# Linear attention with a token mixer: k'v matmuls and q' transposes in 64-row tiles, two PSUM banks each

## The chip, the cores and the metric

The kernel runs on one core of a Trainium2 chip. The metric is the device time of one execution in microseconds (us). Times of a kernel are medians of several executions; a profile is of one execution. Runs come with a state, fast or slow, and with the mean clock that the throttle granted TensorE (1.00 is full speed). On this one core the clock varied from run to run for one and the same kernel: among seven executions of the kernel before on one chip, 177.44 us went with a clock of 0.941 and 185.43 us with 0.892. Fast runs are compared with fast runs. The state is set among runs taken side by side, though: beside e5 to e8 all seven runs of the kernel before lie between 180.51 and 182.86 us (clock 0.897 to 0.926) and count as fast, where runs of that length beside e1 to e4 counted as slow.

## The reference

```python
# attention, per batch (8) and head (8); 576 positions s, 64 dims
q_p = concat(relu(q) * cos_w, relu(q) * sin_w)     # (s, 128), k_p likewise
kv  = einsum('bhsf,bhsd->bhfd', k_p, v)            # contraction over s
z   = sum(k_p, axis=s)
x   = einsum('bhsf,bhfd->bhsd', q_p, kv) / (q_p . z + 1e-6)
# token mixer on x (b, s, 512)
W = (x @ w_q) @ (x @ w_k).T / 8;   out = relu(W @ x) @ w_out
```

## The kernel before

Two heads (a pair) share the 128 partitions: the 576 positions of one head lie on partitions 0 to 63 in nine chunks, those of the other on 64 to 127. To keep the heads apart in a contraction over all 128 rows, `v_ext` holds each head's v beside a block of zeros; a column of ones next to v gives z.

```python
for pr in range(NPAIR):                                  # 4 pairs of heads
    kv_sb = small.tile([P, 2, D + 1], BF16, name="kv_sb")
    qpt_ps = psum.tile([P, C9, P], BF16, name="qpt_ps", bufs=1)        # 2 banks
    kv_ps = psum.tile([P, 2, D + 1], FP32, name="kv_ps", bufs=1)       # 1 bank
    for c in range(C9):                                  # 9 chunks
        nc.tensor.matmul(kv_ps, k_p[:, pr, c, :, :], v_ext[:, pr, c, :, :],
                         start=(c == 0), stop=(c == C9 - 1))
    # (kv_sb <- kv_ps)
    for c in range(C9):
        nc.tensor.transpose(qpt_ps[:, c, :], q_p[:, pr, c, :, :], ident)
    # (qpt_sb <- qpt_ps, on VectorE)
    for hh in range(2):                                  # the two heads
        num_ps = psum.tile([P, SC, D + 1], FP32, name="num_ps", bufs=2)  # 2 banks
        for u in range(SC):                              # 5 slices of 128 positions
            nc.tensor.matmul(num_ps[:, u, :], qpt_sb[:, hh, cb:cb + 2, :],
                             kv_sb[:, hh, :], start=True, stop=True)
        nc.vector.reciprocal(rec, num_ps[:, :, D:D + 1])
        nc.vector.tensor_tensor(x_sb[:, :, h, :], num_ps[:, :, 0:D],
                                rec.to_broadcast([P, SC, D]), op=ALU.mult)
```

The mixer's tiles (`xT_ps`, `moe_ps_a` to `moe_ps_e`) share a pool of three banks. With qpt_ps 2, kv_ps 1 and num_ps 2 all eight banks are taken. A scheduler fixes the order of the instructions on each engine when the kernel is built; on the chip each engine then follows that order.

Of the kernel before, what the change touches and what calls it, by code (L numbers as in the profile page):

```python
# [14 lines left out]
FP32 = mybir.dt.float32  # L15
BF16 = mybir.dt.bfloat16
# [6 lines left out]
def kernel(  # L23
# [10 lines left out]
    nc = tc.nc  # L34

    B, H, S, D = q.shape
    DM = H * D
    DH = moe_w_q.shape[1]
    P = 128
    NPAIR = H // 2  # L40
    C9 = (2 * S) // P
    NDM = DM // P
    SC = S // P + 1
    scale_moe = 1.0 / math.sqrt(DH)

    consts = ctx.enter_context(tc.tile_pool(name="consts", bufs=1))
# [7 lines left out]
    psum = ctx.enter_context(tc.tile_pool(name="psum", bufs=1, space=bass.MemoryType.PSUM))  # L54
# [7 lines left out]
    ident = consts.tile([P, P], BF16)  # L62
# [34 lines left out]

    v_bufs = []
    for i in range(2):
        vb = consts.tile([P, NPAIR, C9, 2, D + 1], BF16, name=f"v_buf{i}")  # L100
        for hh in range(2):
            p0 = hh * 64
            eng = nc.vector if hh == 0 else nc.gpsimd
            eng.memset(vb[p0:p0 + 64, :, :, 1 - hh, :], 0.0)
            eng.memset(vb[p0:p0 + 64, :, :, hh, D:D + 1], 1.0)
        v_bufs.append(vb)

    num_slices = [(i * P, P) for i in range(4)] + [(S - P, P)]
# [3 lines left out]
    def attention(b, x_sb, nsplit):  # L112
        qf = inp.tile([P, NPAIR, C9 * D], FP32, name="qf")
        kf = inp.tile([P, NPAIR, C9 * D], FP32, name="kf")
        vf = inp.tile([P, NPAIR, C9 * D], FP32, name="vf")
        rq = work.tile([P, NPAIR, C9, D], BF16, name="rq", bufs=1)
        rk = work.tile([P, NPAIR, C9, D], BF16, name="rk", bufs=1)
        q_p = work.tile([P, NPAIR, C9, 2, D], BF16, name="q_p")
        k_p = work.tile([P, NPAIR, C9, 2, D], BF16, name="k_p")
        v_ext = v_bufs[b % 2]  # L120

        step = NPAIR // nsplit
        for sp in range(nsplit):
            a, bb = sp * step, (sp + 1) * step
            csb = cossin.unsqueeze(1).to_broadcast([P, step, C9, 2, D])
            for dst, rr, pp, src in ((kf, rk, k_p, k), (vf, None, None, v),
                                     (qf, rq, q_p, q)):
                s4 = src[b].flatten().rearrange(
                    "(pr p e) -> p pr e", pr=NPAIR, p=P)
                nc.sync.dma_start(dst[:, a:bb, :], s4[:, a:bb, :])  # L130
                if rr is None:
                    for hh in range(2):
                        p0 = hh * 64
                        for pr in range(a, bb):
                            nc.gpsimd.tensor_copy(  # L135
                                v_ext[p0:p0 + 64, pr, :, hh, 0:D],
                                dst[p0:p0 + 64, pr, :].rearrange(
                                    "p (c d) -> p c d", c=C9))
                else:
                    nc.any.tensor_scalar(rr[:, a:bb, :, :], dst[:, a:bb, :],  # L140
                                         0.0, None, op0=ALU.max)
                    nc.vector.tensor_mul(  # L142
                        pp[:, a:bb, :, :, :],
                        rr[:, a:bb, :, :].unsqueeze(3).to_broadcast(
                            [P, step, C9, 2, D]),
                        csb)

        for pr in range(NPAIR):
            kv_sb = small.tile([P, 2, D + 1], BF16, name="kv_sb")
            qpt_ps = psum.tile([P, C9, P], BF16, name="qpt_ps", bufs=1)  # L150
            kv_ps = psum.tile([P, 2, D + 1], FP32, name="kv_ps", bufs=1)
            for c in range(C9):
                nc.tensor.matmul(  # L153
                    kv_ps,
                    k_p[:, pr, c, :, :],
                    v_ext[:, pr, c, :, :],
                    start=(c == 0),
                    stop=(c == C9 - 1),
                )
            with tc.high_priority(2000):  # L160
                nc.any.tensor_copy(kv_sb, kv_ps)  # L161
            for c in range(C9):
                nc.tensor.transpose(  # L163
                    qpt_ps[:, c, :], q_p[:, pr, c, :, :], ident)
            qpt_sb = small.tile([P, 2, C9, D], BF16, name="qpt_sb")
            with tc.high_priority(2000):
                nc.vector.tensor_copy(  # L167
                    qpt_sb, qpt_ps.rearrange("f c (hh pp) -> f hh c pp", hh=2))

            for hh in range(2):  # L170
                h = 2 * pr + hh
                num_ps = psum.tile([P, SC, D + 1], FP32, name="num_ps", bufs=2)
                for u in range(SC):
                    cb = cbase_of[u]
                    nc.tensor.matmul(  # L175
                        num_ps[:, u, :],
                        qpt_sb[:, hh, cb:cb + 2, :],
                        kv_sb[:, hh, :],
                        start=True,
                        stop=True,  # L180
                    )
                rec = small.tile([P, SC, 1], FP32, name="rec")
                nc.vector.reciprocal(rec, num_ps[:, :, D:D + 1])
                nc.vector.tensor_tensor(  # L184
                    x_sb[:, :, h, :],
                    num_ps[:, :, 0:D],
                    rec.to_broadcast([P, SC, D]),
                    op=ALU.mult,
                )
# [88 lines left out]
    for b in range(B):  # L278
        x_sb = xpool.tile([P, SC, H, D], BF16, name="x_sb")
        attention(b, x_sb, 4 if b == 0 else 2)  # L280
        if b % 2 == 0:
            mix_sb = mixpool.tile([P, NDM, 2 * S], BF16, name="mix_sb")
            mix_keep = mix_sb
        else:
            mix_sb = mix_keep
        moe_front(b, x_sb, mix_sb, b % 2)
        if b % 2 == 1:
            wout(b - 1, mix_sb)
# [30 lines left out]
```

## Time and profile before

| | before |
|---|---|
| time, first three executions | 177.77 us (176.94 to 178.58) |
| granted clock of the profiled run | 0.932 |
| TensorE (PE) busy | 147.2 us, 83% |
| VectorE (DVE) busy | 134.1 us, 75% |
| ScalarE (ACT), GpSimd (POOL) busy | 89.9 and 56.6 us |

For the argument about buffers, two groups of the page's fifth part are needed too (line, engine, operation, names, shape, count; then busy us, mean ns; then idle time just before them, with what ended it):

```profile
L175 PE MATMUL num_ps<-kv_sb,qpt_sb 128*128 128x65 bf16 x320 | 21.3, 196 | 3.0 <-DVE x_sb L184 1.5
...
L135 POOL CAST v_buf<-vf 64x576 bf16<-64x576 f32 x64 | 51.2, 822 | 71.9 <-DMA vf<-in_v_dram 33.4
```

and a piece of the timeline of the kernel before (start us, us, instruction, count):

```profile
106.16 0.31 PE L175 MATMUL num_ps<-kv_sb,qpt_sb 128*128 128x65 bf16 x5
...
106.55 0.32 PE L175 MATMUL num_ps<-kv_sb,qpt_sb 128*128 128x65 bf16 x5
...
107.00 0.25 DVE L183 RECIPROCAL rec<-num_ps 128x5 f32<-128x5 f32 x2
...
107.21 0.89 DVE L184 TENSOR_TENSOR x_sb<-num_ps,rec 128x320 bf16<-128x320 f32 x2
```

TensorE does both heads of a pair within 0.7 us and hardly ever waits for a division (1.5 us in all). VectorE takes both reciprocals and both products together when it gets to them, 0.84 us after the first head began. Two buffers make that possible.

### The profile page before, as it was taken

The page shows a single profiled execution, that of the slowest core. Times are in us where ns is not written, and L with a number is a line of the kernel's source. Part 1 is how long each engine was busy: PE and PEld are TensorE (multiplying, and loading weights), DVE is VectorE, ACT ScalarE, POOL GpSimd, SP SyncE. Part 2 cuts the span into 40 slices and gives each one's busy share as a digit, 9 for nine tenths or more (in the row PEclk, how much of TensorE's full clock was granted, in tenths as well). Part 3 has the DMA queues.
Part 4 walks back from the last instruction along what each step waited for, and adds up shares of the span by engine and source line. Part 5 has one row for each costly group of instructions (what it writes and reads, how often), then busy time and mean ns, then how long its engine had stood idle before and what let it go on. Part 6 is the DMA issues. An engine that isn't in the chain of part 4 may idle for free.

```text
span 178.0 us, 3706 instructions
## 1 busy us (share of the span) xinstructions
PE 147.2 (83%) x1434; PEld 90.6 (51%) x1434; DVE 134.1 (75%) x279; ACT 89.9 (51%) x167; POOL 56.6 (32%) x75
## 2 busy tenths in 40 slices
PE   6920776889958999999989999998999999759930
PEld 2300774656645446875745467675544756423410
DVE  5827989869999899897799999879994976722000
ACT  3028155148607869525496862491885426033630
POOL 8636283887882300000576000145800000000000
PEclk9995579579999999999999999999999999996996
DMA  6999999999792038789990587999008850000886
GB/s 172 312 393 315 382 397 392 391 392 388 256 387 109 2 80 186 166 220 398 397 385 37 130 204 170 292 400 389 19 0 195 205 135 0 4 0 0 189 201 140
DMA packets 20513, 39.30 MB, mean 221 GB/s; under 512 B 3088, under 2 KB 3088, under 8 KB 20496
## 3 DMA queue, kind: packets, MB, share of 16 engines
q1 hardware_dynamic: 18912, 37.76, 66.7%
q10 hardware_dynamic: 1584, 1.31, 2.5%
q8 instruction: 11, 0.18, 0.4%
q14 instruction: 6, 0.05, 0.1%
HBM read 29.62 MB, written 9.44 MB: 219 GB/s over the span
## 4 chain that ended last, share of the span: by engine, by line
PE 56%; DVE 17%; ACT 10%; DMA 8%; issue 4%; SPq 1%; POOL 0%; ACTq 0%
PE moe_ps_e L260 10%; PE kv_ps L153 10%; PE qpt_ps L163 9%; PE moe_ps_d L242 6%; PE moe_ps_c L229 5%; PE xT_ps L196 5%; PE num_ps L175 5%; DMA qf<-in_q_dram 5%; DVE k_p L142 5%; PE moe_ps_a L207 4%; DVE q_p L142 3%; DVE qpt_sb L167 3%; DVE x_sb L184 3%; ACT wqkT_sb L214 2%; DMA wq_f<-in_moe_w_q_dram 2%
## 5 line engine op out<-in xcount | busy, mean ns | idle before, releaser
L135 POOL CAST v_buf<-vf 64x576 bf16<-64x576 f32 x64 | 51.2, 822 | 71.9 <-DMA vf<-in_v_dram 33.4
L163 PE MATMUL qpt_ps<-ident,q_p 128*128 128x128 bf16 x288 | 29.8, 228 | 10.5 <-DVE q_p L142 9.4
L260 PE MATMUL moe_ps_e<-wo_sb,mix_sb 128*128 128x512 bf16 x144 | 33.9, 391 | 0.3
L153 PE MATMUL kv_ps<-v_buf,k_p 128*128 128x130 bf16 x288 | 29.0, 235 | 2.0 <-ACT kv_sb L161 0.8
L184 DVE TENSOR_TENSOR x_sb<-num_ps,rec 128x320 bf16<-128x320 f32 x64 | 29.8, 481 | 0.1
L167 DVE COPY qpt_sb<-qpt_ps 128x1152 bf16<-128x1152 bf16 x32 | 24.1, 754 | 4.7 <-PE qpt_ps L163 4.2
L268 ACT COPY o_sb<-moe_ps_e 128x512 f32<-128x512 f32 x34 | 19.9, 586 | 13.5 <-PE moe_ps_e L260 7.2
L163 PEld LDWEIGHTS <-q_p 128*128 128x128 bf16 x288 | 19.1, 102 | 14.9 <-DVE q_p L142 10.7
L175 PE MATMUL num_ps<-kv_sb,qpt_sb 128*128 128x65 bf16 x320 | 21.3, 196 | 3.0 <-DVE x_sb L184 1.5
L142 DVE TENSOR_TENSOR k_p<-rk,cossin 128x2304 bf16<-128x2304 bf16 (+1 forms) x18 | 23.3, 1297 | 0.2 <-ACT rk L140 0.2
L140 ACT ACTIVATE rk<-kf 128x1152 bf16<-128x1152 f32 (+1 forms) x17 | 17.7, 1048 | 11.1 <-DVE k_p L142 5.6
L142 DVE TENSOR_TENSOR q_p<-rq,cossin 128x2304 bf16<-128x2304 bf16 (+1 forms) x18 | 23.2, 1290 | 0.0
L260 PEld LDWEIGHTS <-mix_sb 128*128 128x128 bf16 x144 | 14.1, 100 | 17.0 <-issue 2.6
L153 PEld LDWEIGHTS <-k_p 128*128 128x128 bf16 x288 | 19.7, 105 | 5.3 <-ACT kv_sb L161 1.7
L249 ACT ACTIVATE mix_sb<-moe_ps_d 128x512 bf16<-128x512 f32 (+1 forms) x50 | 19.3, 441 | 5.1 <-PE moe_ps_d L242 4.7
L161 ACT CAST kv_sb<-kv_ps 128x130 bf16<-128x130 f32 x24 | 6.4, 268 | 28.0 <-PE kv_ps L153 28.0
L175 PEld LDWEIGHTS <-qpt_sb 128*128 128x128 bf16 x320 | 15.6, 99 | 9.4 <-issue 2.5
L140 ACT ACTIVATE rq<-qf 128x1152 bf16<-128x1152 f32 (+1 forms) x17 | 18.3, 1080 | 3.4 <-DMA qf<-in_q_dram 3.0
L196 PE MATMUL xT_ps<-ident,x_sb 128*128 128x128 bf16 (+1 forms) x160 | 17.4, 220 | 1.3 <-DVE x_sb L184 1.1
L242 PE MATMUL moe_ps_d<-wqkT_sb,kx_sb 64*128 64x512 bf16 x64 | 14.9, 288 | 1.1 <-ACT kx_sb L237 0.7
L201 DVE COPY xT_sb<-xT_ps 128x576 bf16<-128x576 bf16 x32 | 13.4, 441 | 2.4 <-PE xT_ps L196 2.2
L196 PEld LDWEIGHTS <-x_sb 128*128 128x128 bf16 (+1 forms) x160 | 11.6, 99 | 5.1 <-DVE x_sb L184 1.2
(45 smaller groups left out, 103.0 us busy)
## 6 DMA issues: line engine op xcount, KB each, us to landing
out_dram<-o_sb SPq DMA_DIRECT2D x72, 128.0 KB, 2.4
kf<-in_k_dram SPq DMA_DIRECT2D x14, 576.0 KB, 9.5
vf<-in_v_dram SPq DMA_DIRECT2D x14, 576.0 KB, 9.5
qf<-in_q_dram SPq DMA_DIRECT2D x14, 576.0 KB, 10.5
kf<-in_k_dram SPq DMA_DIRECT2D x4, 288.0 KB, 5.4
vf<-in_v_dram SPq DMA_DIRECT2D x4, 288.0 KB, 6.2
qf<-in_q_dram SPq DMA_DIRECT2D x4, 288.0 KB, 7.5
wo_f<-in_moe_w_out_dram ACTq DMA_DIRECT2D x1, 1024.0 KB, 10.7
```

Source lines behind the costliest of these rows:

```text
L135: nc.gpsimd.tensor_copy(v_ext[p0:p0 + 64, pr, :, hh, 0:D], dst[p0:p0 + 64, pr, :].rearrange("p (c d) -> p c d", c=C9))
L140: nc.any.tensor_scalar(rr[:, a:bb, :, :], dst[:, a:bb, :], 0.0, None, op0=ALU.max)
L142: nc.vector.tensor_mul(pp[:, a:bb, :, :, :], rr[:, a:bb, :, :].unsqueeze(3).to_broadcast([P, step, C9, 2, D]), csb)
L153: nc.tensor.matmul(kv_ps, k_p[:, pr, c, :, :], v_ext[:, pr, c, :, :], start=(c == 0), stop=(c == C9 - 1),)
L163: nc.tensor.transpose(qpt_ps[:, c, :], q_p[:, pr, c, :, :], ident)
L167: nc.vector.tensor_copy(qpt_sb, qpt_ps.rearrange("f c (hh pp) -> f hh c pp", hh=2))
L175: nc.tensor.matmul(num_ps[:, u, :], qpt_sb[:, hh, cb:cb + 2, :], kv_sb[:, hh, :], start=True, stop=True,)
L184: nc.vector.tensor_tensor(x_sb[:, :, h, :], num_ps[:, :, 0:D], rec.to_broadcast([P, SC, D]), op=ALU.mult,)
L196: nc.tensor.transpose(xT_ps[:, j0:j0 + npn], x_sb[p0:p0 + npn, u, 2 * hp:2 * hp + 2, :], ident[p0:p0 + npn, p0:p0 + npn],)
L242: nc.tensor.matmul(mx_ps[:, 0:nn], kx_sb[:, dmc * P:(dmc + 1) * P], wqkT_sb[0:64, n0:n0 + nn], start=True, stop=True,)
L260: nc.tensor.matmul(o_ps, mix_sb[:, dmc, rt * P:(rt + 1) * P], wo_sb[:, dmc, :], start=(dmc == 0), stop=(dmc == NDM - 1),)
L268: nc.any.tensor_copy(o_sb, o_ps)
```

## The change

The intent: rows 0 to 63 and 64 to 127 of the array become two tiles that work side by side, one head each. The zeros beside v go, with the memsets that wrote them; 18 casts on all 128 partitions take the place of 64 on 64 partitions; and TensorE should need half the time for kv and the transposes. So that each row tile writes to a bank of its own (the rule is cited in the prediction below), kv_ps gets a second bank, which is taken from num_ps.

```diff
-            eng.memset(vb[p0:p0 + 64, :, :, 1 - hh, :], 0.0)     # and the ones, per half
+        nc.gpsimd.memset(vb[:, :, :, D:D + 1], 1.0)
 ...
-                    for hh in range(2):  ... for pr in range(a, bb):  64-partition casts
+                    nc.gpsimd.tensor_copy(v_ext[:, a:bb, :, 0:D], dst[:, a:bb, :]...)
 ...
-            qpt_ps = psum.tile([P, C9, P], BF16, name="qpt_ps", bufs=1)
-            kv_ps = psum.tile([P, 2, D + 1], FP32, name="kv_ps", bufs=1)
+            qpt_ps = psum.tile([P, 2, 1024], BF16, name="qpt_ps", bufs=1)
+            kv_ps = psum.tile([P, 2, 512], FP32, name="kv_ps", bufs=1)
             for c in range(C9):
-                nc.tensor.matmul(kv_ps, k_p[:, pr, c, :, :], v_ext[:, pr, c, :, :], ...)
+                for hh in range(2):
+                    p0 = hh * 64
+                    nc.tensor.matmul(kv_ps[:, hh, 0:D + 1],
+                                     k_p[p0:p0 + 64, pr, c, :, :],
+                                     v_ext[p0:p0 + 64, pr, c, :], ...)
 ...
-                nc.tensor.transpose(qpt_ps[:, c, :], q_p[:, pr, c, :, :], ident)
+                for hh in range(2):
+                    nc.tensor.transpose(qpt_ps[:, hh, c * D:(c + 1) * D],
+                                        q_p[p0:p0 + 64, pr, c, :, :],
+                                        ident[p0:p0 + 64, p0:p0 + 64])
 ...
-                num_ps = psum.tile([P, SC, D + 1], FP32, name="num_ps", bufs=2)
+                num_ps = psum.tile([P, SC, D + 1], FP32, name="num_ps", bufs=1)
```

More of the change, by code (lines that the diff above doesn't have):

```diff
@@ L99 @@
     for i in range(2):
-        vb = consts.tile([P, NPAIR, C9, 2, D + 1], BF16, name=f"v_buf{i}")
-        for hh in range(2):
-            p0 = hh * 64
-            eng = nc.vector if hh == 0 else nc.gpsimd
-            eng.memset(vb[p0:p0 + 64, :, :, 1 - hh, :], 0.0)
-            eng.memset(vb[p0:p0 + 64, :, :, hh, D:D + 1], 1.0)
+        vb = consts.tile([P, NPAIR, C9, D + 1], BF16, name=f"v_buf{i}")
+        nc.gpsimd.memset(vb[:, :, :, D:D + 1], 1.0)
         v_bufs.append(vb)
@@ L131, in attention @@
                 if rr is None:
-                    for hh in range(2):
-                        p0 = hh * 64
-                        for pr in range(a, bb):
-                            nc.gpsimd.tensor_copy(
-                                v_ext[p0:p0 + 64, pr, :, hh, 0:D],
-                                dst[p0:p0 + 64, pr, :].rearrange(
-                                    "p (c d) -> p c d", c=C9))
+                    nc.gpsimd.tensor_copy(
+                        v_ext[:, a:bb, :, 0:D],
+                        dst[:, a:bb, :].rearrange("p pr (c d) -> p pr c d", c=C9))
                 else:
@@ L149, in attention @@
             kv_sb = small.tile([P, 2, D + 1], BF16, name="kv_sb")
-            qpt_ps = psum.tile([P, C9, P], BF16, name="qpt_ps", bufs=1)
-            kv_ps = psum.tile([P, 2, D + 1], FP32, name="kv_ps", bufs=1)
+            qpt_ps = psum.tile([P, 2, 1024], BF16, name="qpt_ps", bufs=1)
+            kv_ps = psum.tile([P, 2, 512], FP32, name="kv_ps", bufs=1)
             for c in range(C9):
-                nc.tensor.matmul(
-                    kv_ps,
-                    k_p[:, pr, c, :, :],
-                    v_ext[:, pr, c, :, :],
-                    start=(c == 0),
-                    stop=(c == C9 - 1),
-                )
+                for hh in range(2):
+                    p0 = hh * 64
+                    nc.tensor.matmul(
+                        kv_ps[:, hh, 0:D + 1],
+                        k_p[p0:p0 + 64, pr, c, :, :],
+                        v_ext[p0:p0 + 64, pr, c, :],
+                        start=(c == 0),
+                        stop=(c == C9 - 1),
+                    )
             with tc.high_priority(2000):
-                nc.any.tensor_copy(kv_sb, kv_ps)
+                nc.any.tensor_copy(kv_sb, kv_ps[:, :, 0:D + 1])
             for c in range(C9):
-                nc.tensor.transpose(
-                    qpt_ps[:, c, :], q_p[:, pr, c, :, :], ident)
+                for hh in range(2):
+                    p0 = hh * 64
+                    nc.tensor.transpose(
+                        qpt_ps[:, hh, c * D:(c + 1) * D],
+                        q_p[p0:p0 + 64, pr, c, :, :],
+                        ident[p0:p0 + 64, p0:p0 + 64])
             qpt_sb = small.tile([P, 2, C9, D], BF16, name="qpt_sb")
@@ L167, in attention @@
                 nc.vector.tensor_copy(
-                    qpt_sb, qpt_ps.rearrange("f c (hh pp) -> f hh c pp", hh=2))
+                    qpt_sb.rearrange("f hh c pp -> f hh (c pp)"),
+                    qpt_ps[:, :, 0:C9 * D])
             for hh in range(2):
                 h = 2 * pr + hh
-                num_ps = psum.tile([P, SC, D + 1], FP32, name="num_ps", bufs=2)
+                num_ps = psum.tile([P, SC, D + 1], FP32, name="num_ps", bufs=1)
                 for u in range(SC):
```

## The prediction

> **What bounds the kernel now.** I read the page first, for the share of each engine and the chain of work that ended last; then the busy times by stage; then single instructions in the timeline, for the pace of the matmuls that change. The page's first part, its slices of TensorE and its granted clock, and its chain:
>
> ```profile
> PE 147.2 (83%) x1434; PEld 90.6 (51%) x1434; DVE 134.1 (75%) x279; ACT 89.9 (51%) x167; POOL 56.6 (32%) x75
> ...
> PE   6920776889958999999989999998999999759930
> ...
> PEclk9995579579999999999999999999999999996996
> ...
> PE 56%; DVE 17%; ACT 10%; DMA 8%; issue 4%; SPq 1%; POOL 0%; ACTq 0%
> PE moe_ps_e L260 10%; PE kv_ps L153 10%; PE qpt_ps L163 9%; PE moe_ps_d L242 6%; PE moe_ps_c L229 5%; PE xT_ps L196 5%; PE num_ps L175 5%; DMA qf<-in_q_dram 5%; DVE k_p L142 5%; PE moe_ps_a L207 4%; DVE q_p L142 3%; DVE qpt_sb L167 3%; DVE x_sb L184 3%; ACT wqkT_sb L214 2%; DMA wq_f<-in_moe_w_q_dram 2%
> ```
>
> TensorE holds 56% of the chain, and the two groups that change hold 10% and 9% of the span on it, some 34 us. By stage (PE, PEld, DVE, ACT, POOL busy, each with its count, then clock, DMA share and GB/s):
>
> ```profile
> 16.00:32.00 16.00, 10.65 (x127) 9.14 (x127) 15.42 (x31) 6.66 (x10) 8.46 (x11) 0.71 1.04 383
> ...
> 72.00:97.00 25.00, 23.44 (x287) 15.76 (x286) 21.44 (x54) 14.21 (x31) 9.00 (x12) 1.00 0.86 285
> 97.00:131.00 34.00, 32.72 (x353) 20.78 (x352) 30.98 (x63) 20.52 (x42) 8.95 (x12) 1.00 0.69 210
> 131.00:161.00 30.00, 26.80 (x251) 15.37 (x250) 20.26 (x54) 12.64 (x27) 0.00 (x0) 1.00 0.34 80
> ```
>
> From 16 to 32 us VectorE is the bound (15.42 of 16). In the steady stretch of two batches, 97 to 131, TensorE has 32.72 of 34 and VectorE 30.98: nearly level. So a faster TensorE alone can win at most the distance to VectorE, 3 us in 34, and whatever delays VectorE costs in full.
>
> The pace of the matmuls at full clock, from the timeline (start, us, then the group):
>
> ```profile
> 105.14 0.61 PE L163 MATMUL qpt_ps<-ident,q_p 128*128 128x128 bf16 x8
> 106.55 0.32 PE L175 MATMUL num_ps<-kv_sb,qpt_sb 128*128 128x65 bf16 x5
> 71.37 0.63 PE L153 MATMUL kv_ps<-v_buf,k_p 128*128 128x130 bf16 x8
> ```
>
> Less the last one's own length (0.22, 0.19 and 0.22 us by the median rows): (0.61-0.22)/7 = 56 ns for 128 columns, (0.63-0.22)/7 = 58 ns for 130, (0.32-0.19)/4 = 32 ns for 65; the records of single starts give a median of 29 ns for the last. The weight load of 128 columns hides even at 29 ns.
>
> **What the Trainium skill says.** "TensorEngine Tiling (Array Packing)", section Key Properties: tiles work independently, different tiles can load weights and multiply in parallel, and a change of tiling mode drains TensorE. The trace agrees on the drain: between adjacent matmuls it has a median of 152 ns from a 128-row one to a 64-row one and 132 ns back, against 55 and 29 ns within a mode, so about 100 ns a switch. No run here shows the parallel tiles, as the kernel before never alternates two. The same page, section Gotcha 1: PSUM Pressure: different row tiles write to different banks and may not share one. That is what the second bank is for. "TensorE: Matmul & The Clock Gate", section "Wait — 56ns, not 53.3ns?": start to start never falls below about 25 ns however few the columns; the trace's 29 ns for 64 and 65 columns lies just above it. "Perfetto Trace Analysis", section Optimization Strategy: a gap that repeats can mean that PSUM has no room for the next tile. No such gap is in the trace before; I expect it after.
>
> **The change, part by part.**
>
> 1. The kv matmuls and transposes. Removed: 288 x 58 + 288 x 56 ns = 32.8 us of TensorE. Added: 1152 of 65 or 64 columns. If they follow one another like other matmuls of that width, 1152 x 29 ns = 33.4 us: nothing gained, 0.6 us lost. If the two row tiles run side by side, half of that, 16.7 us: 16.1 us of TensorE saved. Which of the two is the main thing that I can't read from this profile. In the slow clock from 13 to 40 us the first kv groups ran at 108 ns each, and side-by-side tiles would help most there, but VectorE and the loads bound that stage.
>
> 2. Mode switches. In the instruction order of the two builds the row mode changes 170 times before and 176 times after: the 64-row work now lies next to transposes of the same mode as often as it parts from the 128-row ones. 6 x 0.1 = 0.6 us, nothing.
>
> 3. The banks. kv_ps grows from one to two, qpt_ps stays at two, moe keeps three, so num_ps falls from two buffers to one. With one, the next head's five matmuls wait until the division of this head is done. The trace gives the links: the reciprocal starts 230 ns after the start of the fifth matmul when VectorE is free, reciprocal and product end 710 ns later, and the next allowed matmul starts 55 ns after; with 120 ns for four starts, 1.1 us a head at least. 64 x 1.1 = 70 us fit in the span only if other work lies between. In the present trace 50 of 63 heads begin before the head in front is divided, so the second buffer is used. In the new order 20 of the 63 gaps between heads hold under 0.5 us of TensorE work, mostly one transpose group (0.38 us), where about 1.0 is needed: 20 x 0.6 = 12 us of TensorE waits at least, and more where VectorE first copies qpt_sb (0.76 us). In a plain attention pair of the new order I followed the steps: qpt ends, copy 0.80, reciprocal and product 0.70, next head; TensorE has 0.6 us of work and stands 0.9. VectorE in turn stands 0.4 us (55+120+230) where two heads follow with nothing between; the order has 13 such places, 5 us.
>
> 4. GpSimd. 64 casts at 822 ns become 4 of 576 and 14 of 1152 elements on all partitions. At the same time per element, 4 x 0.82 + 14 x 1.64 = 26 us instead of 51. It is off the chain, so the saving is small: one wait near 46 us for v_buf (0.7 us on the chain, up to 1.7 with the stretch before it), and four VectorE products of 1.65 to 1.87 us instead of 1.35, and four of 1.0 to 1.2 instead of 0.75, that ran beside casts: half of 3 us. Say 2 us in all.
>
> 5. The start. The two memsets of 2.0 us on VectorE and two of 2.1 on GpSimd vanish, but lie before the loads have landed. The first matmul can be kv after k_p instead of the transpose after q_p, 1.2 us sooner; half of it should remain.
>
> 6. Small shifts. The order gives VectorE 9 more 64-column and 2 more 512-column mix_sb, and 6 more wqkT_sb copies of which one is wide: 9 x 0.22 + 2 x 0.69 + 5 x 0.22 + 0.6 = 5 us, less 3 kv_sb (0.9) and one o_sb (0.7): 3.4 us more, against the 4 us of memsets that bound nothing. The attention of the last batch moves wholly in front of the third output block, so the tail of 22 us before the last block has less to do, and the stretch before it more.
>
> **The sum, for the two cases.** Steady stretch of some 120 us. *Tiles in turn:* +0.6 +0.6, waits for num_ps of 12 us of which I let two thirds reach the end (8, as the rest falls where TensorE waits anyway), VectorE +2, GpSimd -2, start -0.6: about +8, 185 to 186 us. *Tiles side by side:* 16 us of TensorE gone, but VectorE had 105 of those 120 us; with 5 us of standing and 3.4 more work, less 1.5, it has 112 and can't be packed fully: a gain of 2 to 4 us at best from TensorE, 2.6 from items 4 and 5, given back in part to the waits: -2 to -4, 174 to 176 us. I hold them about equally likely.
>
> **The rivals.** First, the full 16 us come through, 165 us. For: the chain holds 34 us of these groups. Against: VectorE's 30.98 of 34, and the chain names only what came last. Second, the single num_ps buffer decides, tiles in turn or not, 184 to 190. For: the 50 of 63 heads. Against: in-order TensorE was given an order made for one buffer, with wide gaps at 43 places. Third, alternating tiles is slower than one mode, as each weight load meets the other tile's matmul; at 40 ns, 46 us instead of 33: over 190. Nothing in the profile speaks for it.
>
> **Range and chances.** The middle of the two cases is 179.5 us, 1% above now. 171.5 holds the side-by-side case with few waits, 188 the other with most of them. The gain of over 2% needs the tiles in parallel and VectorE kept fed: 0.24. Over 2% slower needs tiles in turn, or waits larger than I let through: 0.40. Between them 0.36.
>
> **What would show it.** Start to start inside the new kv groups: 29 ns means in turn, about 15 side by side. TensorE or its weight loads idle on x_sb L184 (1.5 and 2.4 us now): near 12 us shows item 3. VectorE idle before the reciprocal on num_ps (4.3 now): near 9. v_buf casts near 26 us busy. In the stretch of two batches, TensorE well below VectorE in the first case. Wrong would be: casts slower per element, a slower granted clock, or a chain still led by TensorE at a lower total, which would mean that VectorE was less of a bound than I think.

## The result

The changed kernel takes 224.94 us (220.91 to 235.48, four runs) against 178.18 us. Its fast runs are 1.249 times those of before (95% interval 1.229 to 1.268). Such a ratio is the mean time of one kernel's fast runs over that of the other's of the same rounds, so it is not quite the ratio of the medians quoted. The profiled run is slow (226.84 us, clock 0.727), but the two fast runs had 0.730 and 0.741, and a fast run of the first experiment below shows the same structure.

The page after, its first parts and its chain:

```profile
PE 164.8 (73%) x1998; PEld 93.3 (42%) x2010; DVE 138.7 (62%) x289; ACT 87.7 (39%) x153; POOL 25.0 (11%) x27
...
PE   7707565637856889688379997987999779668960
...
PEclk9965555556955899979658999599558955555697
...
PE 44%; DVE 36%; ACT 7%; DMA 6%; issue 3%; SPq 1%; ACTq 0%; DVEq 0%
```

The clock is between one half and six tenths through much of the run, where it was near full speed after the first fifth before. VectorE's part of the chain has doubled from 17% to 36%. TensorE is busy for longer although it has less to do. By stage (columns as in the prediction):

```profile
16.00:32.00 16.00, 10.08 (x257) 8.21 (x259) 16.00 (x24) 7.21 (x11) 3.76 (x4) 0.50 1.02 384
...
97.00:131.00 34.00, 27.21 (x341) 15.81 (x343) 25.88 (x51) 16.96 (x32) 5.85 (x3) 0.82 0.46 159
131.00:161.00 30.00, 25.93 (x410) 15.45 (x410) 18.69 (x52) 7.70 (x17) 0.00 (x0) 0.81 0.26 60
```

From 97 to 131 us neither engine is near full any more: 27.21 and 25.88 of 34, where it was 32.72 and 30.98. So they wait for each other. The table of waits names it (who waited for whom: us in total, times, longest):

```profile
ACT kv_sb L155 <- PE num_ps L174: 37.5, 19, 3.8
...
DVE rec L182 <- PE num_ps L174: 24.3, 17, 9.4
PEld L174 <- DVE x_sb L183: 22.7, 33, 2.0
...
PE num_ps L174 <- DVE x_sb L183: 18.2, 32, 1.8
```

and of the kernel before:

```profile
DVE rec L183 <- PE num_ps L175: 4.3, 5, 2.5
```

TensorE's num_ps matmuls wait 18.2 us for divisions (1.5 before), the reciprocals 24.3 us for num_ps (4.3 before). The first line of the changed kernel is a second-order wait: ScalarE can't store kv_sb until a num_ps matmul has read an older one, as there are six kv_sb tiles and the kv work has run ahead of the heads. A pair in the timeline of the changed kernel:

```profile
91.99 0.47 PE L147 MATMUL kv_ps<-v_buf,k_p 64*128 64x65 bf16 x18 [0.35 <-ACT kv_sb L155]
...
93.19 0.33 PE L174 MATMUL num_ps<-kv_sb,qpt_sb 128*128 128x65 bf16 x5 [0.19 <-DVE x_sb L183]
...
93.55 0.20 DVE L182 RECIPROCAL rec<-num_ps 128x5 f32<-128x5 f32 x1 [0.42 <-PE num_ps L174]
93.78 0.49 DVE L183 TENSOR_TENSOR x_sb<-num_ps,rec 128x320 bf16<-128x320 f32 x1
...
94.33 0.33 PE L174 MATMUL num_ps<-kv_sb,qpt_sb 128*128 128x65 bf16 x5 [0.46 <-DVE x_sb L183]
94.70 0.27 ACT L155 CAST kv_sb<-kv_ps 128x130 bf16<-128x130 f32 x1 [2.27 <-PE num_ps L174]
...
95.02 0.54 PE L147 MATMUL kv_ps<-v_buf,k_p 64*128 64x65 bf16 x18 [0.36 <-ACT kv_sb L155]
```

Two things are to be seen. The tiles do work side by side: 18 matmuls in 0.47 us, less the last one's 0.20, is 16 ns from start to start, and (0.46-0.20)/17 = 15 ns in another group. That is the pace of the quickest groups: over the 24 kv groups that the trace has whole, the median is 26 ns, as 16 of them ran at a clock near 0.5. And the heads stand in a row: VectorE idle 0.42, TensorE idle 0.46, in turn, with 1.14 us from one head to the next and 3.03 us from one pair to the next. Early in the run it is worse, as VectorE's order has other work inside a division:

```profile
26.71 0.43 PE L174 MATMUL num_ps<-kv_sb,qpt_sb 128*128 128x65 bf16 x5 [0.38 <-DVE x_sb L183]
...
28.38 0.18 DVE L182 RECIPROCAL rec<-num_ps 128x5 f32<-128x5 f32 x1
28.48 1.31 DVE L134 TENSOR_TENSOR k_p<-rk,cossin 128x2304 bf16<-128x2304 bf16 x1
...
29.72 0.75 DVE L165 COPY qpt_sb<-qpt_ps 128x1152 bf16<-128x1152 bf16 x1
...
30.39 0.47 DVE L183 TENSOR_TENSOR x_sb<-num_ps,rec 128x320 bf16<-128x320 f32 x1
...
30.96 0.45 PE L174 MATMUL num_ps<-kv_sb,qpt_sb 128*128 128x65 bf16 x5
```

This head holds the buffer from 26.71 to 30.86, over 4 us.

I therefore tallied the hold in every trace: from the start of a head's first num_ps matmul to the end of the instruction that reads the buffer last.

| profiled run | num_ps buffers | mean hold | 64 holds together | next head begun before the hold ended |
|---|---|---|---|---|
| before | 2 | 2.90 us | 186 us | 50 of 63 |
| changed | 1 | 2.13 us | 136 us | 0 |
| before with one buffer (e1) | 1 | 2.09 us | 134 us | 0 |
| changed, division first (e8) | 1 | 1.77 us | 113 us | 0 |
| changed, ScalarE empties it (e7) | 1 | 1.12 us | 71 us | 0 |

With one buffer the holds can't overlap, so 136 us of the 224.8 are taken by them in a row, besides the stages in which no head is at work at all. From the first num_ps matmul to the last product it is 132.7 us before, 170.5 in e1 and 178.2 in the changed kernel: nearly all of the loss lies in the stretch of the heads. With two buffers the holds overlap, and together they cover only 113.6 us. They are also longer, as TensorE runs ahead of VectorE: between the fifth matmul and the reciprocal lie 86 us in all before and 45 in e1.

### The profile page after: what moved, and what is told of

Read it like the earlier page. It is cut to its first block, busy times and chain, and to the rows that moved or that the text cites. A ratio compares the mean times of both kernels' runs of the same rounds, so it can differ in the third digit from the quotient of the medians.

```text
span 224.8 us, 4796 instructions
## 1 busy us (share of the span) xinstructions
PE 164.8 (73%) x1998; PEld 93.3 (42%) x2010; DVE 138.7 (62%) x289; ACT 87.7 (39%) x153; POOL 25.0 (11%) x27
## 4 chain that ended last, share of the span: by engine, by line
PE 44%; DVE 36%; ACT 7%; DMA 6%; issue 3%; SPq 1%; ACTq 0%; DVEq 0%
PE moe_ps_e L259 14%; DVE x_sb L183 9%; DVE q_p L134 8%; DVE qpt_sb L165 7%; PE num_ps L174 7%; PE moe_ps_c L228 7%; DVE k_p L134 6%; PE moe_ps_a L206 6%; PE moe_ps_d L241 4%; PE xT_ps L195 4%; DMA qf<-in_q_dram 3%; ACT mix_sb L248 3%; DVE rec L182 3%; DVE xT_sb L200 2%; PE kv_ps L147 2%
## 5 line engine op out<-in xcount | busy, mean ns | idle before, releaser
L174 PE MATMUL num_ps<-kv_sb,qpt_sb 128*128 128x65 bf16 x320 | 26.5, 219 | 19.1 <-DVE x_sb L183 18.2
L128 POOL CAST v_buf<-vf 128x1152 bf16<-128x1152 f32 (+1 forms) x18 | 23.9, 1325 | 100.0 <-PE kv_ps L147 42.6
L147 PE MATMUL kv_ps<-v_buf,k_p 64*128 64x65 bf16 x576 | 22.7, 220 | 14.4 <-DVE k_p L134 10.5
L183 DVE TENSOR_TENSOR x_sb<-num_ps,rec 128x320 bf16<-128x320 f32 x64 | 31.1, 486 | 1.3
L159 PE MATMUL qpt_ps<-ident,q_p 64*128 64x64 bf16 x576 | 25.1, 216 | 6.7 <-DVE qpt_sb L165 5.4
L174 PEld LDWEIGHTS <-qpt_sb 128*128 128x128 bf16 x320 | 17.3, 111 | 29.4 <-DVE x_sb L183 22.7
L182 DVE RECIPROCAL rec<-num_ps 128x5 f32<-128x5 f32 x64 | 12.0, 188 | 24.5 <-PE num_ps L174 24.3
L147 PEld LDWEIGHTS <-k_p 64*128 64x128 bf16 x576 | 16.4, 112 | 20.2 <-DVE k_p L134 11.8
L155 ACT CAST kv_sb<-kv_ps 128x130 bf16<-128x130 f32 x27 | 7.2, 266 | 43.1 <-PE num_ps L174 37.5
L195 PE MATMUL xT_ps<-ident,x_sb 128*128 128x128 bf16 (+1 forms) x160 | 20.7, 252 | 3.9 <-DVE x_sb L183 3.4
L159 PEld LDWEIGHTS <-q_p 64*128 64x128 bf16 x576 | 18.5, 110 | 11.1 <-issue 6.7
L248 ACT ACTIVATE mix_sb<-moe_ps_d 128x512 bf16<-128x512 f32 (+1 forms) x39 | 17.2, 484 | 8.5 <-PE moe_ps_d L241 6.5
```

The lines of the kernel that those rows point to most:

```text
L128: nc.gpsimd.tensor_copy(v_ext[:, a:bb, :, 0:D], dst[:, a:bb, :].rearrange("p pr (c d) -> p pr c d", c=C9))
L147: nc.tensor.matmul(kv_ps[:, hh, 0:D + 1], k_p[p0:p0 + 64, pr, c, :, :], v_ext[p0:p0 + 64, pr, c, :], start=(c == 0), stop=(c == C9 - 1),)
L159: nc.tensor.transpose(qpt_ps[:, hh, c * D:(c + 1) * D], q_p[p0:p0 + 64, pr, c, :, :], ident[p0:p0 + 64, p0:p0 + 64])
L195: nc.tensor.transpose(xT_ps[:, j0:j0 + npn], x_sb[p0:p0 + npn, u, 2 * hp:2 * hp + 2, :], ident[p0:p0 + npn, p0:p0 + npn],)
L248: nc.any.tensor_scalar(mix_sb[:, dmc, half * S + n0: half * S + n0 + nn], mx_ps[:, 0:nn], scale_moe, 0.0, op0=ALU.mult, op1=ALU.max,)
```

## The experiments

Theory A: the lost num_ps buffer, with the order built for it, costs the time. Theory B: the 64-row tiles themselves do. No run separates the wait for the buffer from the order that the scheduler builds around one buffer; theory A takes both together. Labels run from e1 to e16. All results were correct. The table has the medians, the ratio of the fast runs, and from the profiled run the clock and TensorE's busy time; the last column is their product, a crude measure of the clocked work that TensorE did. The profiled runs of the changed kernel, e2, e5, e6, e8, e10, e11 and e16 are slow, so their clock and busy time are not those of a fast run.

| run | kernel | median us | ratio | clock | PE busy | busy x clock |
|---|---|---|---|---|---|---|
| before | | 178.18 | 1 | 0.932 | 147.2 | 137 |
| changed | | 224.94 | 1.249 | 0.727 | 164.8 | 120 |
| e1 | before, num_ps 1 | 220.94 | 1.236 | 0.835 | 164.1 | 137 |
| e2 | changed, num_ps 2, moe 2 | 192.72 | 1.079 | 0.807 | 156.6 | 126 |
| e3 | before, moe 2 | 192.08 | 1.078 | 0.893 | 153.6 | 137 |
| e4 | only transposes tiled | 186.83 | 1.039 | 0.905 | 147.9 | 134 |
| e5 | changed, tiles in turn | 225.99 | 1.200 (one fast run) | 0.699 | 178.5 | 125 |
| e6 | e4, tiles in turn | 192.17 | 1.032 | 0.853 | 163.9 | 140 |
| e7 | changed, ScalarE empties num_ps | 189.68 | 1.019 (one fast run) | 0.873 | 149.5 | 131 |
| e8 | changed, division first | 211.86 | 1.136 (one fast run) | 0.764 | 161.1 | 123 |
| e9 | before, num_ps 1, ScalarE empties | 191.46 | 1.068 | 0.900 | 152.7 | 137 |
| e10 | before, num_ps 2, ScalarE empties | 190.17 | 1.060 | 0.886 | 152.8 | 135 |
| e11 | e7 with 4 SBUF tiles | 191.49 | 1.044 (one fast run) | 0.815 | 155.2 | 126 |
| e12 | e11 with filling | 205.28 | 1.147 | 0.914 | 159.8 | 146 |
| e13 | before, 5 output buffers | 184.72 | 1.029 | 0.903 | 149.4 | 135 |
| e14 | before, 2 rk buffers | 183.21 | 1.009 | 0.932 | 146.9 | 137 |
| e15 | e9, 3 output buffers | 192.41 | 1.075 | 0.911 | 150.9 | 137 |
| e16 | e11, 3 output buffers | 195.62 | 1.062 (one fast run) | 0.778 | 163.7 | 127 |

### One part alone: the lost buffer

```diff
-  num_ps = psum.tile([P, SC, D + 1], FP32, name="num_ps", bufs=2)    # kernel before
+  num_ps = psum.tile([P, SC, D + 1], FP32, name="num_ps", bufs=1)
```

> The kernel before with one num_ps buffer instead of two, nothing else: no row tiles, a bank left free. Theory A (the lost num_ps buffer makes the heads follow one another, with the order built for it, and the idle TensorE is then granted a slower clock): 205 to 225 us, clock 0.70 to 0.80, VectorE idle before the reciprocal 15 us or more. Theory B (the 64-row tiles themselves, by their alternation or by the little work they give TensorE, lower the clock and cost the time): 177 to 182 us, clock 0.93.

220.94 us. Fast runs have 1.236 times the time of before, against 1.249 for the whole change. Theory A holds and B falls; only the clock, 0.835, is above the 0.70 to 0.80 that A gave. Its page and waits, of a fast run:

```profile
PE 164.1 (75%) x1434; PEld 98.9 (45%) x1434; DVE 145.6 (67%) x290; ACT 87.5 (40%) x156; POOL 67.8 (31%) x75
...
ACT kv_sb L161 <- PE num_ps L175: 31.1, 17, 3.6
...
DVE rec L183 <- PE num_ps L175: 19.9, 18, 7.0
...
PE num_ps L175 <- DVE x_sb L184: 14.2, 21, 1.6
```

They are the waits of the changed kernel, without a row tile in it. Of the 40.7 us that its span is longer, 16.9 are TensorE busy for longer, and the lower clock agrees with that: 147.2 x 0.932 / 0.835 = 164.3, measured 164.1. The other 23.8 us are TensorE not busy.

### The buffer given back, from another pool

```diff
-  ... name="num_ps", bufs=1)      tag="moe", bufs=3)     # changed kernel
+  ... name="num_ps", bufs=2)      tag="moe", bufs=2)     # e3: the kernel before, moe 2 only
```

> The changed kernel with num_ps at two buffers again and the bank taken from the moe tiles (three to two). Theory A: most of the 47 us come back, 172 to 188 us, less what two moe buffers cost, which the next run measures on the kernel before. Theory B: 210 us or more.

> The kernel before with two moe buffers instead of three, as a control for the run with both. Both theories say the same here: 178 to 186 us, as each output block waits for a copy of 0.59 us against 0.86 us of matmuls, which two buffers mostly cover.

192.72 and 192.08 us. Most of the loss is gone, as A says, though 192.72 is above its 172 to 188. The reason is in the control: it lost as much by the smaller moe pool (7.8%, more than the 0 to 4% that I expected). So at equal buffers the row tiles are worth nothing here. The page's first line of each, e2 and then e3:

```profile
PE 156.6 (81%) x2010; PEld 88.2 (46%) x2010; DVE 130.3 (67%) x288; ACT 87.4 (45%) x154; POOL 22.6 (12%) x27
```

```profile
PE 153.6 (81%) x1434; PEld 92.3 (48%) x1434; DVE 135.5 (71%) x290; ACT 88.3 (46%) x156; POOL 55.6 (29%) x75
```

TensorE is busy no less with the tiles than without them (e2's page is of a slow run), at a clock of 0.839 to 0.847 in the fast runs of e2 against 0.893 to 0.910 in e3.

### Only the transposes

```diff
 # kernel before, with the changed kernel's qpt_ps ([P, 2, 1024]), transposes and qpt_sb copy;
 # kv_ps, v_ext and num_ps (bufs=2) as before: no bank is lost
```

> Only the q' transposes in two alternating row tiles, which need no more than the two banks that qpt_ps has already; kv as before, num_ps at two, moe at three. Theory A: no buffer lost, so faster by part of the 8 us of TensorE that the transposes free (288 x 56 ns down to 576 x 15): 172 to 178 us. Theory B: slower by half of the loss of the whole change, 195 to 205 us, with a clock below 0.85.

186.83 us, 1.039: neither faster, as A had it, nor within B's 195 to 205. The order of its instructions changes the row mode 234 times, against 170 before: each transpose group now lies between 128-row work. At the 0.1 us a change that the prediction read from the trace, 64 more cost 6.4 us, as much as the tiles save on the transposes (288 x 56 ns less 576 x 17 ns, 6.3 us). That is a reckoning, not a test; a part of the 3.9% is also the order itself (e13 below).

### Without the alternation

```diff
-            for c in range(C9):
-                for hh in range(2):
+            for hh in range(2):
+                for c in range(C9):
```

> The changed kernel with the loops over chunk and head exchanged, so that nine matmuls of one row tile are followed by nine of the other; every engine's instruction order has the same shape, and only the alternation is gone. Pace expected 29 ns instead of 15 at full clock. Theory A (the heads' chain through the one num_ps buffer bounds): no more than 5 us slower than the changed kernel, 1.23 to 1.28 times the kernel before, although TensorE has 8 to 16 us more to do. Theory C (TensorE's time is what counts, and the alternation saves it): 1.30 times or more.

> The same exchange in the kernel that tiles only the transposes (186.8 us, where the order of the instructions has 64 more changes of row mode than the kernel before: 234 against 170). If its small loss is 64 mode changes at 0.1 us, 6.4 us, set off by what the alternation saves, 288 x 56 ns less 576 x 17 ns or 6.3 us, then without alternation 576 x 12 ns or 7 us more of TensorE: 188 to 194 us, 1.04 to 1.07 times before. If TensorE doesn't bound there either: the same as with alternation, 1.02 to 1.03.

These are clean pairs: the instructions of every engine keep their sequence of shapes. The pace changed as meant, though not to 29 ns: the quickest kv groups of e5 have 26 ns from start to start (16 in the changed kernel), the quickest q' groups of e6 23 (15 in e4). Nine matmuls of one tile and then nine of the other (e5) took 225.99 us against 224.94, and its one fast run was even the lower, 218.57. (The ratio, 1.200, is under A's 1.23 to 1.28, as the kernel before was slower beside e5.) So what the alternation saves is of no use in the changed kernel, where the heads' chain bounds, as A says. On the transposes alone (e6) the two fast runs took 186.97 and 188.63 us, 1.032 times before; those of e4, taken earlier on the same chip, 184.48 and 185.82, 1.039 times before. The times say a little slower and the ratios a little faster, so no difference can be told, and the reckoning above stays untested.

### A shorter hold

```diff
+                num_sb = small.tile([P, SC, D + 1], FP32, name="num_sb")
+                with tc.high_priority(2000):
+                    nc.scalar.copy(num_sb, num_ps)       # then reciprocal and product from num_sb
```

> The changed kernel with one num_ps buffer, but ScalarE first copies it to a tile in SBUF and VectorE divides from there. The buffer is then held for some 0.23 + 0.45 us instead of 0.23 + 0.71 and for whatever VectorE puts before or between the two division instructions. Theory A': it is the hold by VectorE's queue that costs: 180 to 200 us. If one buffer alone, however short its hold, forces the slow order: 210 us or more.

> The changed kernel with reciprocal and product at high priority in the scheduler, so that VectorE does them as soon as they are ready and not after k_p, q_p or qpt_sb instructions; the buffer count stays at one. Theory A': if VectorE's other work between num and division (up to 3.2 us of hold in the first heads) is the main part: 190 to 205 us. If the bare chain of 1.1 us a head and the kv and q' work running ahead is: 215 us or more.

With one buffer still, but emptied by a ScalarE copy, the kernel takes 189.68 us, and 185.54 in its one fast run: most of the loss comes back. The ratio 1.019 flatters it, as the kernel before took 182.1 us beside it; against the 178.2 beside e1 it is 1.041. The copy's group:

```profile
L183 ACT COPY num_sb<-num_ps 128x325 f32<-128x325 f32 x64 | 27.6, 431 | 16.8 <-PE num_ps L174 12.0 <-ACT num_sb L183 1.8 <-DVE x_sb L186 1.5
```

Moving only VectorE's division to the front (e8) shortens the holds from 136 to 113 us and gives 211.86 us, between the two answers. So it is the length of the hold that one buffer makes expensive; how much of it falls to VectorE's other work inside the hold and how much to the bare chain, e8 does not tell.

### What the row tiles are worth when no buffer is lost to them

```diff
 # e9:  kernel before, num_ps bufs=1, ScalarE's copy (num_sb bufs=4); one bank unused
 # e10: the same with num_ps bufs=2
 # e11: e7 with num_sb bufs=4 (same instruction order as e7)
 # e12: e11 and, ahead of each kv group:
+            for _ in range(2):
+                for hh in range(2):
+                    p0 = hh * 64
+                    nc.tensor.matmul(kv_ps[:, hh, :], k_p[p0:p0 + 64, pr, 0, :, :],
+                                     wo_sb[p0:p0 + 64, 0, :], start=True, stop=True)
```

> The kernel before (no row tiles) with one num_ps buffer and ScalarE's copy of it to SBUF (four such tiles); the bank that this frees stays unused. If the length of the hold is what one buffer costs, also here: 180 to 192 us instead of 220. Against the changed kernel with the same copy, run beside it, it tells what the row tiles are worth when no buffer is lost to them: theory D (nothing, as their mode changes, 218 against 176 in the orders, and the slower clock eat it): within 1.5%. Theory E (the 16 us of TensorE come through in part): the changed kernel with the copy is faster by 2% or more.

> The kernel before with both num_ps buffers and ScalarE's copy: a possible better kernel, as ScalarE has room and TensorE waits less for the division; but VectorE, near its limit, gains nothing and its product reads SBUF at 533 ns instead of 481, 64 x 52 ns = 3.3 us more. Expected 176 to 183 us, 0.97 to 1.01 times before.

> The changed kernel with ScalarE's copy of num_ps as in the earlier run, with four SBUF tiles for it instead of six so that it has the same as the two kernels beside it; the order of instructions is the same as with six. Expected the same again, 1.02 to 1.06 times before. Theory D and E as told at the first of these runs.

> The same kernel with four more row-tile matmuls of 512 columns at the head of each kv group, whose results the group overwrites: 32 x 2 x 0.216 us, 14 us of TensorE work at full clock that nothing needs. If the slower granted clock takes back what the row tiles save, busier TensorE gets a higher clock (0.87 to 0.90 or more) and the time changes by less than 1% or falls. If TensorE simply bounds it: 8 to 14 us slower than without the filling.

e9 and e11 have the same median, 191.46 and 191.49 us, but all of e9's runs count as fast and five of e11's six as slow. The one fast run of e11, 187.0, is 2.3% under the fast runs of e9, just over the 2% that I had set for theory E, but it is one run. So the tiles are worth between nothing and some 2%, not the 16 us of TensorE. The clock in fast runs is 0.860 against 0.886 to 0.900.

e10 was hoped to be better than the kernel before and is 6% slower: a miss. The cause was not tested; VectorE is busy for 148.1 us instead of 134.1, and its product, read from SBUF, takes 605 ns instead of 481. But e9 and e10 together show how much the hold counts: once ScalarE empties num_ps, fast runs take 191.3 us with one buffer and 189.9 with two, 0.8% apart, where without the copy the second buffer is worth 24%.

e12 raised the clock as meant, to 0.914, but at 205.28 us the question stays open: the scheduler made a different order from it (TensorE's weight loads waited 15.1 us for qpt_sb, which e11's ten longest waits don't have), so the edit did more than fill. Between 20 and 60 us its clock was 0.98 against 0.63 in e11's slow profile and 0.65 in the fast one of e7, which has e11's order. Its first output block began at 59.6 us, against 63.7 and 62.1, filling included: a hint, no more.

A rival to the clock as the reason why the tiles bring so little is VectorE. The stretch from 20 to 60 us in e9 and then e11 (columns as in the prediction):

```profile
20.00:60.00 40.00, 31.04 (x388) 22.18 (x385) 38.36 (x76) 26.47 (x53) 29.91 (x30) 0.93 0.89 330
20.00:60.00 40.00, 33.35 (x506) 21.35 (x507) 36.71 (x74) 22.98 (x45) 8.58 (x7) 0.63 0.87 334
```

VectorE is busy for 38.4 and 36.7 of these 40 us, more than TensorE, so a TensorE with less to do has little to win there. Mode changes are a second rival: the orders have 218 against 176 (e11, e9) and 232 against 168 (e16, e15 below). No run separates these three.

### How much is the order's luck?

```diff
 # e13: kernel before, outpool bufs 4 -> 5     # e14: kernel before, rk bufs 1 -> 2
 # e15: e9, outpool bufs 4 -> 3                # e16: e11, outpool bufs 4 -> 3
```

> The kernel before with one more output buffer (five for four), which by itself can cost nothing; but the scheduler makes a rather different order from it (0.74 alike on TensorE, 0.66 on VectorE). Theory F (the order that the scheduler happens to make is worth several per cent, and the kernel before has a lucky one): 183 to 190 us, 1.03 to 1.07. Theory G (the order matters little; what the other kernels lost came from their edits): 0.99 to 1.02.

> The same test with another harmless edit: two rk buffers for one, and an order 0.52 and 0.36 alike. Theory F: 183 to 192 us, 1.03 to 1.08; theory G: 0.98 to 1.02.

> The kernel without row tiles, one num_ps buffer and ScalarE's copy (1.068 times before), with three output buffers instead of four, so that it gets another order (0.63 alike). With its twin, the next run, a second pair of with and without row tiles. Expected 186 to 197 us, clock 0.89; TensorE busy time times clock 137 us as in all kernels without tiles.

> The changed kernel with ScalarE's copy and three output buffers: the tiled twin of the run before it. Theory D (the work that the tiles save is taken back by a slower granted clock): the same time as its twin within 2%, clock 0.80 to 0.85, TensorE busy time times clock 120 to 128 us, busy time alone the same. Theory E (the tiles are worth their 16 us, and the first pair hid it by its orders): faster than the twin by 4% or more.

One buffer more, of which I expect no cost by itself, made the kernel before 2.9% slower (interval 1.8 to 4.0) or left it within noise (0.9%, interval -0.7 to 2.5). So an order can be worth some 3%, and losses of that size in e4 and e6 must not be laid to their edits alone. The third pair, e15 and e16: fast runs 190.7 and 190.5 us (one alone in e16), medians 192.41 and 195.62, clocks of fast runs 0.903 to 0.911 and 0.840. In three pairs with three sorts of order the tiles brought 0%, 2% and 0%. No kernel with row tiles ran faster than the kernel before.

In the last column of the table every kernel without row tiles stands at 135 to 137 and the kernels with both parts tiled and alternating at 120 to 131 (e12 has its filling besides), while busy time is no shorter in the slow profiles, and 3 us shorter in the one fast profile of such a kernel beside its like (e7 149.5, e9 152.7). The tiles do take clocked work from TensorE, and the granted clock is lower by about as much. That the lower clock is what takes the gain back agrees with all pairs but was not shown by an intervention, as the filling changed the order; VectorE and the mode changes, named above, may have a part in it.

## Why the prediction was wrong

It gave 179.5 us, a range of 171.5 to 188, and its rival with the single buffer 184 to 190. Measured: 224.94.

- **Item 3, the banks, is the step that failed: what the lost buffer costs.** The mechanism is right; 50 of 63 heads do use the second buffer, and e1 has the loss without a row tile. The size is off: of "20 x 0.6 = 12 us of TensorE waits at least" 8 were let through to the time, and e1 measures 42 us (fast runs 220.3 against 178.2). The direct wait was not so far off: TensorE's num_ps matmuls wait 14.2 us for divisions in e1 and 18.2 in the changed kernel. Two terms were too small all the same. I counted only the gaps under 0.5 us, though a head needs about 1.0: with the changed kernel's order and the prediction's own paces, 32 to 43 of the 63 gaps fall short, by 18 to 24 us in all (an estimate). And I set the hold of a head at its bare minimum, 1.1 us. It also has what VectorE's order puts into it: its mean is 2.13 us, 3.0 in the first 16 heads; of the 136 us some 33 lie before the reciprocals beyond the 0.23 us each, and 22 between the start of a reciprocal and the end of its product, beyond 0.71 each.
- **What follows from the waits was not in the sum.** The kv_sb tiles fill up and ScalarE waits 37.5 us for num_ps (31.1 in e1); and the clock is lower, 0.835 in e1, without a tile, and 0.727 in the changed kernel, for 0.932. The prediction listed "a slower granted clock" among what would make it wrong but gave it no time. In e1 TensorE is busy 16.9 us longer, of 40.7. That idler TensorE is why the clock was lower was not tested.
- **Item 1, the pace, was right in its second case:** 15 to 16 ns at full clock, "about 15 side by side". The "2 to 4 us at best" that it was to bring stand beside 0 to 2% in the matched pairs, so they are neither shown nor refuted; of the 16 us of the first rival no pair shows more than some 4 (e11, one run).
- **Item 2, the mode changes:** 176 against 170 in the order, and nothing in the comparison points to them. Where they rose by 64 (e4), they may have cost what the tiles saved.
- **Item 4, GpSimd:** casts of 23.9 us, 26 predicted. The relief for VectorE did not come: with casts beside them single k_p and q_p products still took up to 2.08 us, and the mean of the long q_p ones is 1544 ns against 1393 before. In e7's profile, with the same casts, it is 1342.
- **Item 5, the start:** the first kv matmul came at 16.96 us instead of the first transpose at 18.83, 1.9 us sooner, but the first output block began at 81.0 us instead of 62.2 (82.9 in e1), so nothing of it can be seen.
- **The signs that it named** came true in kind: x_sb as TensorE's releaser (18.2 us; "near 12" was given), VectorE idle before the reciprocal (24.5; "near 9").

## What to carry to other kernels

Before a buffer is taken away, add up how long each use holds it in the trace as it is, from the first write to the end of the last read. Here 64 holds made 186 us on two buffers, more than the span of 178, where the bare chain of 1.1 us a head made 70. The sum is a warning and no forecast: with one buffer the same holds shrank to 134 us (e1), and the rule was not tried on another kernel. When a change frees an engine at the price of a buffer, first try the loss of the buffer alone: it took one word here and gave nearly all of the loss. If the buffer must go, shorten the hold with an engine that has room (e7, e9); here that still left 2 to 7% over the kernel before. And TensorE time that is freed is not yet time saved: in all three pairs here the granted clock was lower with the tiles, and the kernel won 0 to 2%.

## What the Trainium skill lacked or had wrong

- "TensorE: Matmul & The Clock Gate", section "Wait — 56ns, not 53.3ns?", gives about 25 ns as the least time from one matmul's start to the next, however small the matmul. Within one tile that agrees with the runs (29 ns); between two alternating row tiles it doesn't: 18 matmuls of 65 columns started 15 to 16 ns apart on average at full clock. The page treats tiles that run at once in a part of its own, so the sentence is worded too widely rather than the case missing.
- "TensorEngine Tiling (Array Packing)", section Key Properties, is right that tiles work in parallel, and says that a change of mode drains TensorE, but not what it costs: about 100 ns in this trace (152 and 132 ns between starts, against 55 and 29).
- No page that I read says whether packed tiles change the clock that a kernel is granted. In fast runs it was 0.839 to 0.847 with tiles and 0.893 to 0.910 without (e2, e3), 0.860 and 0.886 to 0.900 (e11, e9), 0.840 and 0.903 to 0.911 (e16, e15). The orders of these pairs differ too, so the runs do not show the tiles alone to be the reason.
- "Perfetto Trace Analysis", section Optimization Strategy, has the sign of a missing buffer, the repeating gap, but no way to tell ahead what a buffer is worth. The sum of the holds, 186 us on two buffers in a span of 178, would have been a warning here.
